# The gate job of one group of LayerNorm moments, and the GpSimd transfer behind it, one job later in the key sweep

## The chip, the core and the metric

The kernel runs on one core of a Trainium2 chip. A core has five engines with instruction streams of their own: PE (TensorE, the matmuls), DVE (VectorE), ACT (ScalarE), POOL (GpSimd) and SP (SyncE, which here only issues transfers). They wait for one another by semaphores. Transfers between the core's memory and DRAM are carried out by 16 DMA engines; SP, ACT and POOL only issue them. The metric is the device time of one execution in microseconds (us); the median of three runs is compared.

## The reference

The input `x` has 2048 rows (tokens) of 576 numbers. The output mixes two blocks with a gate per token:

```python
def _A_ref(x, wqkv, wo):                       # linear attention, 32 heads of 18
    q, k, v = split of (x @ wqkv) into heads
    pq, pk = phi(q), phi(k)                    # phi(t) = t+1 if t>0 else exp(t), + 1e-6
    kv  = einsum("bhsd,bhse->bhde", pk, v)     # sums over all tokens
    z   = einsum("bhsd->bhd", pk)
    o = einsum("bhqd,bhde->bhqe", pq, kv) / (einsum("bhqd,bhd->bhq", pq, z) + 1e-6)
    return o @ wo

def _B_ref(x, w1, b1, w2, b2):                 # per token: LayerNorm, Dense(4608), GELU, Dense(576)
    y = _layernorm(x)                          # (x - mean) / sqrt(var + 1e-5)
    return gelu(y @ w1 + b1) @ w2 + b2

g = sigmoid((x * gate_w).sum(-1, keepdims=True))
out = g * _A_ref(x, ...) + (1 - g) * _B_ref(x, ...)
```

## The kernel before

**Tiles and stages.** The 2048 tokens are 16 tiles of 128. The kernel first sweeps over the tiles (the key sweep, up to about 187 us of the span), then forms the attention weights, attends tile by tile, and spends the rest, from about 280 us to the end at 1120 us, in the two dense layers of block B, whose order a planner sets. Only the key sweep matters here. It visits the tiles in the order `ORDER`; below, step n is the n-th tile visited (n from 0), and the main loop runs steps 3 to 15.

**One step of the sweep** (the loop at L582). PE projects the tile on the key weights in two halves of 14 matmuls each (called KEY(n) below, 28 matmuls `ps<-y 128x288`), multiplies parts of step n-1 (`add_products`, `ps<-xs,ks` and `ps<-ks,xs`), projects on the query weights (again 28 matmuls `ps<-y`, called QUERY(n)), and adds the other products of step n-1. The two PSUM banks 6 and 7 take the halves in turn, KEY half 0, KEY half 1, QUERY half 0, QUERY half 1, so each half must be read out before the projection two halves later may write. The read-out of a half is two ACT activations (tile `e`) and one DVE instruction, `k<-ps,e` for keys and `accs<-ps,e` (or `acc<-ps,e`) for queries. ACT and DVE also split the next `x` tile (`y<-t`), the finished keys (`ks<-k`) and the tile in its other layout (`xs<-xn`) into a high and a low part; ACT takes the sum of squares of step n-1 (`xn<-xn,nmean`).

**Transfers.** SP issues, in program order, the next `x` tile (`t<-in_xm`, `t<-in_xe` twice; three steps ahead), its row layout (`xn<-in_x`; one step ahead) and what the jobs below ask for. SP issues in order: what waits holds up all behind it. Each of SP's transfers uses one of eight semaphores in turn and waits until the transfer eight places ahead has landed.

**The jobs.** Between the pieces of a step three lists of small jobs are run: list 3n behind `split_xn` of step n and ahead of QUERY(n)'s read-out, list 3n+1 behind that read-out, list 3n+2 at the step's end, ahead of KEY(n+1)'s read-out. They are written into each engine's stream in that place. Two sorts of jobs matter.

*Gates* (L347 to L385): for a group b of tiles (`MOMENTS`, L34; group 0 is the first two tiles visited, group 1 the third and fourth, and so on) `gates_in` (three DVE instructions of two columns), `gates_act` (on ACT: an Exp, a Sqrt and an Exp, with two loads of function tables), `gates_out` (eight small DVE instructions) and `share_moments`, in which POOL issues a transfer that writes the group's means and reciprocal deviations (tile `mr`, 128 partitions of four numbers) to DRAM (`moments`), turned around so that each of the 512 numbers goes to a place of its own.

*Pairs* (`Y_JOBS`, L83): for a pair j of tiles `load_pair` has SP load the pair's moments back, repeated in all partitions (`accs<-moments`), and the tiles themselves (`accs<-in_xm`, `accs<-in_xe` twice, for each of the two tiles). `normal_pair` (DVE, four instructions `accs<-accs 128x768`) normalizes them, then sums, splits (`ys`, `y`) and stores (`yd<-ys`) follow, for block B. Pair 0 needs group 0's moments: it is loaded in list 13 and normalized in lists 16 (two instructions) and 17 (two). Pair 1 needs group 1's: loaded in list 20, normalized in 22 and 23.

The list number of each group's gates is set in L561; list 12 belongs to step 4 and list 15 to step 5:

```python
    for b, n in enumerate((9, 12, 22, 28)):
        at(n, gates_in, b)
        at(n + 1, gates_act, b)
        at(n + 2, gates_out, b)
        at(n + 2, share_moments, b)
```

All instructions go through a helper, so the profile gives nearly all of them line L111; they are told apart by their tiles.

Of the kernel before, what the change touches and what calls it, by code (L numbers as in the profile page):

```python
# [114 lines left out]
def tile_gated_mix(ctx: ExitStack, tc: tile.TileContext, x, xm, xe, wm, we, wvm, wve, wo, um, ue, w2, b1, b2, gw, out):  # L115
# [68 lines left out]
    for part in (KEY, QUERY):  # L184
        for half in range(2):
            n = HALF + 2 * (part == KEY and half)
# [360 lines left out]
    def at(n, f, *args):  # L547
        jobs[n].append(lambda: f(*args))
# [9 lines left out]
    at(3 * 5, sp.dma_start, b1s, b1)  # L558
    at(9, load_wv)
    at(40, load_wo)  # L560
    for b, n in enumerate((9, 12, 22, 28)):  # L561
        at(n, gates_in, b)
        at(n + 1, gates_act, b)
        at(n + 2, gates_out, b)
        at(n + 2, share_moments, b)
# [956 lines left out]
```

## Time and profile before

| | us |
|---|---|
| median of three runs | 1126.16 (1124.97 to 1127.82) |
| the profiled execution, its own time | 1122.1 |
| its span | 1120.4 |
| PE busy in the span | 1105.2 |
| mean granted TensorE clock | 0.998 |

The profile is of one execution. Its span begins with the first instruction. "Idle before" is time in which an engine waited, with what ended the wait. In a timeline the number behind x tells how many equal instructions a row merges, so that a row's duration can hold more than one of them. DMA rows have two sides: the row on SPq or POOLq is the issue, and the transfer lands later. PE is busy nearly throughout, so what counts is the few places at which it isn't, and the granted clock behind them.

### The profile page before, as it was taken

The numbers are of one execution on the slowest core, as the hardware profiler recorded it, in microseconds if no ns is written. First come the engines' busy times: TensorE is split into PE (matmuls) and PEld (weight loads), VectorE is DVE, ScalarE is ACT, GpSimd is POOL, SyncE is SP. The second block draws the span as 40 slices with busy tenths as digits, with TensorE's granted clock in tenths as the row PEclk, the third lists the DMA queues.
The fourth block names the chain that finished last, engine by engine and source line by source line (L and its number), as shares of the span: only waits on it lengthen the run. The fifth ranks groups of instructions, "written<-read, shape, count | busy, mean of one in ns | idle before, by whom it ended". The sixth has DMA issues, their size and how long they took to land.

```text
span 1120.4 us, 18589 instructions
## 1 busy us (share of the span) xinstructions
PE 1105.2 (99%) x6766; PEld 1007.0 (90%) x6766; DVE 890.9 (80%) x1381; ACT 648.4 (58%) x1158; POOL 396.2 (35%) x326
## 2 busy tenths in 40 slices
PE   9989999999999999999999999999999999999998
PEld 9989999999888888898988889888999899889898
DVE  5558785796787979879988987887887788878888
ACT  6657765354556665676756666445554555455542
POOL 2111112431334252544515353325443444344430
PEclk9999999999999999999999999999999999999999
DMA  6475673745636546473564649774445444444432
GB/s 184 122 94 177 165 202 110 265 176 193 202 133 209 194 162 202 143 268 118 209 211 156 225 155 349 291 250 130 117 127 146 126 120 127 137 127 127 119 111 85
DMA packets 108862, 189.42 MB, mean 169 GB/s; under 512 B 8924, under 2 KB 68588, under 8 KB 104674
## 3 DMA queue, kind: packets, MB, share of 16 engines
q1 hardware_dynamic: 107858, 187.49, 52.7%
q8 instruction: 53, 0.87, 0.3%
q10 hardware_dynamic: 720, 0.74, 0.2%
q14 instruction: 39, 0.32, 0.1%
q0 software_dynamic: 192, 0.01, 0.0%
HBM read 121.40 MB, written 66.80 MB: 168 GB/s over the span
## 4 chain that ended last, share of the span: by engine, by line
PE 80%; DVE 10%; DMA 4%; issue 2%; ACT 2%; SPq 1%; POOL 1%; ACTq 0%; DVEq 0%; POOLq 0%
PE ps L111 80%; DVE accs L111 3%; DVE h L111 2%; DVE region L111 1%; DMA accs<-in_xe 1%; SPq L111 1%; DVE wa L111 1%; DMA w1d<-wb 1%; DMA fresh<-in_ue 1%; DVE wb L111 1%; DVE u L111 1%; POOL fresh L111 1%; ACT u L111 0%; DMA s<-in_wm 0%; DMA fresh<-in_w 0%
## 5 line engine op out<-in xcount | busy, mean ns | idle before, releaser
L111 PEld LDWEIGHTS ps<-region,h 128*128 128x128 f32 x3144 | 454.8, 188 | 43.5 <-DVE accs L111 7.2
L111 PE MATMUL ps<-region,h 128*128 128x288 f32 x3144 | 479.4, 295 | 5.4 <-DVE accs L111 2.3
L111 DVE TENSOR_TENSOR accs<-ps,accs 128x576 f32<-128x576 f32 x336 | 250.5, 753 | 88.4 <-PE ps L111 83.7
L111 POOL TENSOR_TENSOR fresh<-fresh 128x288 f32<-128x288 f32 (+1 forms) x164 | 172.2, 1057 | 374.2 <-DMA fresh<-in_w 258.2
L111 PE MATMUL ps<-y,wa 128*128 128x512 f32 x1008 | 269.0, 393 | 0.4 <-DVE wa L111 0.4
L111 PE MATMUL ps<-y,wb 128*128 128x512 f32 x756 | 203.9, 396 | 0.2 <-ACT u L111 0.2
L111 PEld LDWEIGHTS ps<-y,wa 128*128 128x128 f32 x1008 | 176.7, 188 | 25.5 <-DVE wa L111 1.1
L111 POOL TENSOR_TENSOR u<-u 128x512 f32<-128x512 f32 x104 | 163.3, 1570 | 96.9 <-DVE h L111 59.4
L111 DVE TENSOR_TENSOR h<-u,h 128x512 fp32r<-128x512 f32 x222 | 187.3, 858 | 3.7 <-ACT u L111 3.0
L111 PEld LDWEIGHTS ps<-y,wb 128*128 128x128 f32 x756 | 132.6, 188 | 23.4 <-ACT u L111 0.8
L111 PE MATMUL ps<-y 128*128 128x288 f32 (+1 forms) x896 | 127.5, 299 | 4.7 <-DVE k L111 4.3
L111 PEld LDWEIGHTS ps<-y 128*128 128x128 f32 x896 | 123.9, 191 | 6.8 <-DVE k L111 4.7
L111 ACT ACTIVATE u<-ps 128x512 f32<-128x512 f32 x73 | 43.7, 599 | 145.2 <-PE ps L111 145.2
L111 DVE TENSOR_TENSOR region<-fresh,region 128x576 fp32r<-128x576 f32 x120 | 97.1, 809 | 2.0 <-ACT region L111 1.6
L111 ACT ACTIVATE region<-fresh 128x576 fp32r<-128x576 f32 x120 | 74.1, 630 | 36.7 <-PE ps L111 31.9
L111 ACT ACTIVATE h<-ps,b1s 128x512 fp32r<-128x512 f32 x45 | 30.9, 686 | 77.0 <-PE ps L111 76.9
L111 ACT ACTIVATE h<-u,b1s 128x512 fp32r<-128x512 f32 x73 | 52.6, 721 | 32.0 <-DVE u L111 31.2
L111 ACT ACTIVATE h<-u 128x512 fp32r<-128x512 f32 x104 | 60.3, 620 | 16.1 <-POOL u L111 16.0
L111 PE MATMUL ps<-wp,qt 128*128 128x288 f32 x448 | 63.3, 298 | 0.0
L111 DVE TENSOR_TENSOR wa<-fresh,wa 128x512 fp32r<-128x512 f32 x64 | 47.9, 749 | 18.8 <-ACT wa L111 17.9
L111 DVE TENSOR_TENSOR u<-ps,u 128x512 f32<-128x512 f32 x74 | 50.9, 688 | 14.8 <-ACT u L111 12.8
L111 POOL TENSOR_TENSOR pks<-pks,k 128x576 f32<-128x576 f32 x15 | 21.9, 1459 | 111.8 <-DVE k L111 111.8
(122 smaller groups left out, 1040.7 us busy)
## 6 DMA issues: line engine op xcount, KB each, us to landing
w1d<-wa SPq DMA_DIRECT2D x17, 1280.0 KB
wa<-w1d SPq DMA_DIRECT2D x68, 320.0 KB
fresh<-in_w SPq DMA_DIRECT2D x70, 288.0 KB
y<-yd SPq DMA_DIRECT2D x14, 1280.0 KB
w1d<-wb SPq DMA_DIRECT2D x17, 960.0 KB
wb<-w1d SPq DMA_DIRECT2D x51, 320.0 KB
yd<-ystage SPq DMA_DIRECT2D x28, 320.0 KB
fresh<-in_um SPq DMA_DIRECT2D x64, 128.0 KB
```

Source lines behind the costliest of these rows:

```text
L111: return lambda *args, **kwargs: self.tc.keep_in_program_order(op(*args, **kwargs))
```

## The change

One number of L561: the jobs of group 1 go from lists 12, 13 and 14 (all in step 4) to lists 13, 14 and 15. The transfer by POOL goes from list 14 to list 15, which is in step 5.

```diff
-    for b, n in enumerate((9, 12, 22, 28)):
+    for b, n in enumerate((9, 13, 22, 28)):
         at(n, gates_in, b)
         at(n + 1, gates_act, b)
         at(n + 2, gates_out, b)
         at(n + 2, share_moments, b)
```

No instruction is added or removed. The streams of PE, ACT and SP stay as they were, word for word; DVE's and POOL's change. In the rows below `mr_108` is group 1's tile, `moments_113` and `moments_114` are groups 0 and 1 in DRAM.

DVE at the end of step 4: `gates_in` of group 1 (the three rows without a sign), then what stands behind it.

```order
+L111 SCALAR_TENSOR_TENSOR accs<-ps,e 128x288 x2
 L111 COPY mr_108<-nmean 128x2
 L111 TENSOR_SCALAR mt<-sumsq 128x2
 L111 TENSOR_SCALAR g<-gsum 128x2
-L111 SCALAR_TENSOR_TENSOR accs<-ps,e 128x288 x2
+L111 SCALAR_TENSOR_TENSOR k<-ps,e 128x288
+L111 TENSOR_TENSOR y<-t,y 128x512
+L111 TENSOR_TENSOR y<-t,y 64x128
+L111 SCALAR_TENSOR_TENSOR k<-ps,e 128x288
+L111 SCALAR_TENSOR_TENSOR ks<-k,ks 128x576
+L111 TENSOR_TENSOR xs<-xn,xs 128x512
+L111 TENSOR_TENSOR xs<-xn,xs 128x64
```

`gates_in` stood ahead of the two read-outs of QUERY(4) and now stands behind them; behind it DVE goes on at once with step 5.

DVE at the end of step 5: the last instruction of group 1's `gates_out`, and what follows it, up to `normal_pair` of pair 0 (the last row).

```order
 L111 TENSOR_SCALAR mt<-mt 128x2
 L111 TENSOR_TENSOR mr_108<-mr_108,mt 128x2
-L111 SCALAR_TENSOR_TENSOR k<-ps,e 128x288
-L111 TENSOR_TENSOR y<-t,y 128x512
-L111 TENSOR_TENSOR y<-t,y 64x128
-L111 SCALAR_TENSOR_TENSOR k<-ps,e 128x288
-L111 SCALAR_TENSOR_TENSOR ks<-k,ks 128x576
-L111 TENSOR_TENSOR xs<-xn,xs 128x512
-L111 TENSOR_TENSOR xs<-xn,xs 128x64
 L111 SCALAR_TENSOR_TENSOR accs<-ps,e 128x288 x2
 L111 TENSOR_TENSOR accs<-accs 128x768 x4
```

`gates_out` stood ahead of step 5's seven key-side instructions and now stands behind them, directly ahead of the read-outs of QUERY(5) and of pair 0's normalizing.

POOL: the running sum of the keys (`pks`, one instruction a step) and the transfers of the moments.

```order
 L111 TENSOR_TENSOR pks<-pks,k 128x576
 L111 DMA moments_113<-mr_107 128x4x1
-L111 TENSOR_TENSOR pks<-pks,k 128x576
+L111 TENSOR_TENSOR pks<-pks,k 128x576 x2
 L111 DMA moments_114<-mr_108 128x4x1
-L111 TENSOR_TENSOR pks<-pks,k 128x576 x4
+L111 TENSOR_TENSOR pks<-pks,k 128x576 x3
 L111 DMA moments_115<-mr_109 128x4x1
```

The transfer of group 1 moved behind step 5's key sum; group 0's stays where it was.

## The prediction

> **What bounds the kernel now.** I read the chain of waits first, then who waits for whom in the key sweep, then the timelines of PE, DVE and SP where PE stands still, and the transfers by windows last. The page's chain, and the longest waits of PE and of DVE for a transfer between 30 and 230 us (us in total, times, longest):
>
> ```profile
> PE 80%; DVE 10%; DMA 4%; issue 2%; ACT 2%; SPq 1%; POOL 1%; ACTq 0%; DVEq 0%; POOLq 0%
> PE ps L111 <- DVE k L111: 4.3, 1, 4.3
> DVE accs L111 <- DMA accs<-in_xe: 6.1, 2, 5.8
> ```
>
> PE is the bound; in the whole sweep it stands still once. PE's timeline shows where (start, us; the 28 matmuls `ps<-y` are KEY or QUERY):
>
> ```profile
> 61.20 3.90 PE L111 MATMUL ps<-y 128*128 128x288 f32 x28
> 66.69 3.88 PE L111 MATMUL ps<-y 128*128 128x288 f32 x28
> 72.40 3.90 PE L111 MATMUL ps<-y 128*128 128x288 f32 x28
> ...
> 82.40 5.46 PE L111 MATMUL ps<-y 128*128 128x288 f32 x28 [4.35 <-DVE k L111]
> 89.69 3.90 PE L111 MATMUL ps<-y 128*128 128x288 f32 x28
> 100.89 3.90 PE L111 MATMUL ps<-y 128*128 128x288 f32 x28
> 112.09 3.90 PE L111 MATMUL ps<-y 128*128 128x288 f32 x28
> ```
>
> KEY(5) starts at 61.20, KEY(6) at 72.40, KEY(7) at 89.69, KEY(8) at 100.89, KEY(9) at 112.09. A step takes 11.20 us, but step 6 takes 17.29. So 6.09 us are lost in it: 4.35 us of idle PE ahead of QUERY(6), and 1.58 us more because QUERY(6) takes 5.46 us instead of 3.88 (the rest, 0.16, is between the two readings). The second part is the clock, by the window that holds QUERY(6) (the 0.57 is the granted clock):
>
> ```profile
> 82.00:86.00 4.00, 3.60 (x16) 3.60 (x17) 3.11 (x6) 2.08 (x3) 1.42 (x1) 0.57 0.22 69
> ```
>
> The cause of the idle time, followed back: the chain's own row, and DVE's instruction that ends PE's wait.
>
> ```profile
> 66.57 13.33 DMA accs<-in_xe
> 81.90 0.46 DVE k L111
> ```
>
> QUERY(6) waits for a bank that DVE reads out at 81.90 (`k<-ps,e`); ahead of it in DVE's stream stands `normal_pair` of pair 0, which waits for the pair's last `accs<-in_xe`, 13.33 us on its way. Why so slow? Here are POOL's four transfers of moments (groups 0 to 3), the time from issue to landing of the four, and windows of 5 to 8 us with the DMA engines' busy share and the GB/s moved as their last two numbers:
>
> ```profile
> 51.98 0.82 POOL L111 DMA_DIRECT2D moments<-mr  x1 [6.17 <-DVE mr L111]
> 63.19 0.78 POOL L111 DMA_DIRECT2D moments<-mr  x1 [6.17 <-DVE mr L111]
> 111.43 0.77 POOL L111 DMA_DIRECT2D moments<-mr  x1 [2.99 <-DVE mr L111]
> 134.38 0.77 POOL L111 DMA_DIRECT2D moments<-mr  x1 [2.99 <-DVE mr L111]
> DMA to landing us min/median/max: 10.5/11.6/12.7
> ```
>
> ```profile
> 56.00:64.00 8.00, 8.00 (x59) 7.87 (x58) 4.25 (x16) 6.27 (x13) 1.80 (x2) 1.00 0.82 25
> 64.00:68.00 4.00, 4.00 (x27) 3.69 (x26) 2.30 (x5) 3.66 (x10) 1.21 (x1) 1.00 0.95 165
> 68.00:76.00 8.00, 8.00 (x59) 7.87 (x58) 2.48 (x5) 3.34 (x8) 0.21 (x1) 1.00 0.70 36
> 90.00:98.00 8.00, 8.00 (x57) 7.69 (x57) 6.31 (x13) 6.39 (x15) 1.44 (x1) 1.00 0.82 236
> 118.00:123.00 5.00, 5.00 (x37) 4.89 (x36) 3.82 (x9) 3.23 (x7) 1.11 (x1) 1.00 0.83 27
> 139.00:145.00 6.00, 6.00 (x41) 5.71 (x41) 4.79 (x10) 4.47 (x12) 1.43 (x1) 1.00 0.71 28
> ```
>
> Four times, from 4 to 7 us behind POOL's issue until 11 to 13 us behind it, everything moves at 25 to 36 GB/s with engines 70 to 83% busy; between these stretches it is 165 to 236. I call this the stretch of a group. Group 1's (issue 63.19, stretch to 76) falls on pair 0's loads, which SP issues from 62.98 on:
>
> ```profile
> 62.98 0.34 SPq L111 DMA_DIRECT2D accs<-moments  x1
> ...
> 68.39 7.60 SPq L111 DMA_DIRECT2D t<-in_xm  x1
> ```
>
> SP itself is caught behind them: 7.60 us on `t<-in_xm` for step 8, and all that it issues next. (The 62.98 is not group 1's doing: the first row waits for group 0's moments, issued 11.0 us before.)
>
> **The change, part by part.** *`gates_in` and `gates_act`.* `gates_in` goes behind the read-outs of QUERY(4), so ACT's first Exp waits for it. Groups 2 and 3 already stand in this phase of a step; the nearest rows are group 2's Exp and, in the second fence, group 3's end of step 10 with KEY(11) and KEY(12), which has `gates_out`, two read-outs and four normalizing instructions in the order that step 5 gets:
>
> ```profile
> 100.72 0.20 ACT L111 ACTIVATE g<-g 128x2 f32<-128x2 f32 x1 [0.74 <-DVE g L111]
> ```
>
> ```profile
> 134.51 4.01 PE L111 MATMUL ps<-y 128*128 128x288 f32 x28
> 145.82 3.90 PE L111 MATMUL ps<-y 128*128 128x288 f32 x28
> 134.74 3.80 DVE L111 TENSOR_TENSOR accs<-accs 128x768 f32<-128x768 f32 x4
> 138.46 0.45 DVE L111 SCALAR_TENSOR_TENSOR k<-ps,e 128x288 f32<-128x288 f32 x1
> ```
>
> ACT waits 0.74 us; queued behind it are KEY(8)'s read-out and all of ACT's next step. Yet KEY(8) to KEY(9) is 11.20 us: a plain step. Cost 0; its cover is PE's work between KEY's first half and QUERY's, and without it the cost would be those 0.74 us.
>
> *`gates_out`.* Eight instructions move behind step 5's key side; QUERY(5)'s read-outs wait for them, and KEY(6) for these. KEY(11) to KEY(12) takes 11.31 us in that order: 0.11 us over a plain step. I take 0.11; the ends are 0 (the row of KEY(8)) and 0.74.
>
> *The transfer on POOL.* It goes past one key sum, which nobody waits for soon. Group 2's left 10.54 us behind its step's KEY (111.43 - 100.89), so group 1's would leave at 61.20 + 10.54 = 71.7. Its stretch, now from 67 or 68 to 76, is then from 75 or so to 71.7 + 12.7 = 84.4.
>
> *Pair 0's loads.* SP's order is unchanged and group 0's landing too, so they leave from 62.98 as before. By the shapes in the code the pair is 1.02 MB (256 KB of repeated moments, and 256 and twice 64 KB for each tile). Up to 68 us 0.66 MB have been moved (165 GB/s for 4 us); at 236 GB/s the rest is there by 69.6, at 165 by 70.2. In step 10 DVE reached `normal_pair` 0.23 us behind KEY(11)'s start (134.74 - 134.51), so here at about 72.6. So DVE's wait of 6.1 us goes whole; KEY(6) is read out 3.95 us behind its start as KEY(11) was (138.46), and QUERY(6) starts 5.49 us behind KEY(6) as QUERY(5) did (66.69 - 61.20).
>
> *What is late next.* Behind pair 0 SP issues step 8's `x` tile (0.32 MB), step 6's row layout `xn` (0.29 MB) and step 9's tile (0.32 MB). At 236 GB/s from 69.6 on, `xn` is there at 72.2, ahead of the stretch. ACT's use of `xn` in steps 6 and 7:
>
> ```profile
> 84.45 0.67 ACT L111 ACTIVATE xs<-xn 128x576 fp32r<-128x576 f32 x1
> ...
> 95.95 0.68 ACT L111 ACTIVATE xs<-xn 128x576 fp32r<-128x576 f32 x1
> ```
>
> In step 7 that is 6.26 us behind KEY(7), so in step 6 it would be at 72.40 + 6.26 = 78.7. Step 9's tile may be caught; it has until step 8. Step 7's `xn` is issued into the stretch at about 78 and lands by 85 or 86 (0.29 MB at 236 GB/s behind its end); step 7 uses it at 83.7 + 6.26 = 90.0. Then pair 1: SP waits for group 1's landing, 84.4 at the latest, instead of issuing at 89.29, less the 6.0 that everything is earlier, or 83.3.
>
> ```profile
> 89.29 0.41 SPq L111 DMA_DIRECT2D accs<-moments  x1
> 100.60 3.81 DVE L111 TENSOR_TENSOR accs<-accs 128x768 f32<-128x768 f32 x4
> ```
>
> That leaves 100.60 - 6.0 - 84.4 = 10.2 us until its normalizing, against 11.3 that were enough, and the 4.3 to 6.2 us that 1.02 MB take at 236 or 165 GB/s. Cost 0.
>
> *Sum.* 17.29 - 11.20 - 0.11 = 5.98 us less in step 6, all of it on PE's path, and nothing in the streams behind is tied to an absolute time: 1122.1 - 6.0 = 1116.1 us for the profiled execution. It lies 4.1 us below the median of the runs; applied to that, 1126.2 - 6.0 = 1120.2. No row tells what those 4.1 us are; were they a longer wait at the same place, the gain could reach 10 us.
>
> **The skill, weighed.** The page "DMA: Bandwidth & Descriptors" of the Trainium skill, in its section on the anatomy of one DMA on the SWDGE (gpsimd) path, gives such a transfer 2.0 us and its bytes at 436 GB/s. By that, the 2 KB of a group would be gone 2 us after the issue, the slow stretches would not be theirs, and the change would gain nothing (the third rival); the 10.5 to 12.7 us measured here decide against it. The page "TensorE: Matmul & The Clock Gate", in its section on what is actually happening, has the clock halve after an idle window of about 3.4 us. Pair 0's 4.35 us idle with its 0.57 agrees, and by that rule a rest of the wait under 3.4 us would cost only itself.
>
> **The rivals.** *First, a rest of the wait stays:* pair 0 lands 1 to 4 us after 72.6, or `xn` is caught in part. DVE has little room in step 6, so most of it comes back on PE: gain 2 to 5 us, 1121.2 to 1124.2. For it: SP's semaphores let a late transfer hold the eighth behind it. Against: 2.4 us between landing and need.
>
> *Second, the stretch hits step 6's `xn` whole, and the kernel gets slower.* The transfer then lands when the stretch ends, 84.4; from ACT's use of it (84.45) to KEY(7) (89.69) there are 5.24 us of work, so KEY(7) would start at 89.6, and with the 1.58 us of the slow clock the sweep would stand 1.5 us worse than now: 1127.7. It is slower from a landing of 82.9 on, and by 0.3% (3.4 us, about what a measurement of this kernel can tell from no change) from 86.3 on. For it: group 1's issue at 71.7 comes before the 72.2 at which `xn` has landed, and only the 4 to 7 us from issue to stretch keep them apart. Against: group 3's issue at 134.38 stood 2.6 us behind an `xn` (131.75), and KEY(11) to KEY(12) is 11.31 us:
>
> ```profile
> 131.75 0.52 SPq L111 DMA_DIRECT2D xn<-in_x  x1
> ```
>
> *Third, the stretches aren't the transfers':* pair 0's loads are slow by themselves, and nothing changes: 1126.2. Against: four stretches for four issues, and pair 1's loads at 236 GB/s.
>
> **How the numbers follow.** Forecast 0.73 (1118.5 to 1121.5 by itself), first rival 0.11, second 0.09, third 0.07. Faster by over 0.3% is the forecast and half of the first rival: 0.78. Slower by over 0.3% is the second with a landing beyond 86.3, and something unforeseen: 0.07. The rest, 0.15, is within. The range goes from 1116.5 (part of the unexplained 4.1 us gained as well) to the far end of the first rival, 1124.2.
>
> **What would show it.** Right: PE has no wait for `k` near 78 us and the clock stays at 1.00; KEY(6) to KEY(7) takes about 11.3 us; `normal_pair` follows the read-outs without a wait; a stretch at 25 to 40 GB/s lies between 75 and 84 instead of 68 and 76. Wrong: ACT waits at `xs<-xn` for the transfer near 79 us (the second rival), or DVE at pair 0's `normal_pair` in spite of full speed before 72 (the third), or DVE there by a few us or at pair 1's near 94 (the first).

## The result, and the profile after

The changed kernel is faster, by less than 1%. In the first comparison its median is 1116.43 us (1116.29 to 1119.06), that of the kernel before 1125.57 (1124.13 to 1127.82), four runs each: a ratio of 0.9923, with a 95% interval from 0.9900 to 0.9945. In later sets with far more runs, on three chips, the gain is smaller: 0.9974 [0.9963, 0.9985] and 0.9970 [0.9956, 0.9984] on the two that ran both kernels (below). Two executions were disturbed and are left out of all figures below: one of 2189.58 us in e5, and one of 5120.93 us in e9, the one that was profiled there.

| profiled execution | before | after |
|---|---|---|
| its own time, us | 1122.1 | 1116.29 |
| its span, us | 1120.4 | 1114.6 |
| mean granted clock | 0.998 | 1.000 |
| KEY(6) to KEY(7), us | 17.29 | 11.20 |

The span is 5.8 us shorter. Followed by the start of PE's n-th matmul, which is the same matmul in both traces, the kernel before is 0.5 us ahead up to KEY(6), 5.6 us behind from KEY(7) on (89.69 against 84.07), and 5.8 us behind at the last matmul. So in this pair of traces the whole gain lies in step 6.

PE's longest wait between 30 and 230 us, and its timeline (start, us; KEY(5), QUERY(5), KEY(6), QUERY(6), KEY(7), KEY(8)):

```profile
PE ps L111 <- DVE wp L111: 0.2, 1, 0.2
```

```profile
61.67 3.90 PE L111 MATMUL ps<-y 128*128 128x288 f32 x28
67.16 3.88 PE L111 MATMUL ps<-y 128*128 128x288 f32 x28
72.87 3.90 PE L111 MATMUL ps<-y 128*128 128x288 f32 x28
78.36 3.88 PE L111 MATMUL ps<-y 128*128 128x288 f32 x28
84.07 3.90 PE L111 MATMUL ps<-y 128*128 128x288 f32 x28
95.27 3.90 PE L111 MATMUL ps<-y 128*128 128x288 f32 x28
```

The 4.35 us ahead of QUERY(6) are gone, QUERY(6) takes 3.88 us at full clock instead of 5.46, and each of these steps is a plain one of 11.20 us. The 0.2 us that is left belongs to another place (`wp`).

The rows of the other engines on which the prediction's steps stood, from the timelines of ACT (the Exp of group 1, and step 6's use of `xn`), DVE (`normal_pair` of pair 0 and of pair 1), POOL (group 1's transfer) and SP (pair 1's moments), and the time from issue to landing of the four transfers of moments:

```profile
61.50 0.20 ACT L111 ACTIVATE g<-g 128x2 f32<-128x2 f32 x1 [0.74 <-DVE g L111]
79.12 0.68 ACT L111 ACTIVATE xs<-xn 128x576 fp32r<-128x576 f32 x1
72.58 3.81 DVE L111 TENSOR_TENSOR accs<-accs 128x768 f32<-128x768 f32 x4
94.97 3.81 DVE L111 TENSOR_TENSOR accs<-accs 128x768 f32<-128x768 f32 x4
72.22 0.78 POOL L111 DMA_DIRECT2D moments<-mr  x1 [2.99 <-DVE mr L111]
83.88 0.41 SPq L111 DMA_DIRECT2D accs<-moments  x1
DMA to landing us min/median/max: 10.1/10.5/10.8
```

And the windows, with granted clock, DMA share and GB/s as the last three numbers:

```profile
68.00:76.00 8.00, 8.00 (x58) 7.87 (x58) 7.22 (x17) 3.79 (x9) 2.02 (x2) 1.00 0.74 199
76.00:84.00 8.00, 8.00 (x53) 7.57 (x52) 6.80 (x15) 6.51 (x15) 1.42 (x1) 1.00 0.51 22
84.00:90.00 6.00, 6.00 (x42) 5.67 (x41) 4.94 (x11) 4.31 (x11) 0.35 (x1) 1.00 0.79 271
```

From 68 to 76 us, where the kernel before moved 36 GB/s, 199 are moved now: pair 0's loads and the `xn` of step 6 pass ahead of the stretch. The slow stretch has gone behind the transfer, to 76 to 84 us (22 GB/s), and there nothing that is in flight is needed soon: DVE's `normal_pair` at 72.58 and ACT's `xs<-xn` at 79.12 show no wait for a transfer.

### The profile page after: what moved, and what is told of

Same layout as the page of the kernel before. It is cut to its first block, busy times and chain, and to the rows that moved or that the text cites. A ratio compares the mean times of both kernels' runs of the same rounds, so it can differ in the third digit from the quotient of the medians.

```text
span 1114.6 us, 18587 instructions
## 1 busy us (share of the span) xinstructions
PE 1102.9 (99%) x6766; PEld 1004.2 (90%) x6766; DVE 890.6 (80%) x1381; ACT 647.6 (58%) x1158; POOL 398.2 (36%) x326
## 4 chain that ended last, share of the span: by engine, by line
PE 77%; DVE 11%; DMA 5%; ACT 2%; issue 2%; SPq 2%; POOL 1%; ACTq 0%; DVEq 0%; POOLq 0%
PE ps L111 77%; DVE accs L111 3%; DVE h L111 2%; DVE region L111 2%; SPq L111 2%; DMA w1d<-wb 1%; DMA fresh<-in_ue 1%; DVE wb L111 1%; ACT u L111 1%; DVE wa L111 1%; DMA yd<-ystage 1%; DMA accs<-in_xe 1%; DVE u L111 1%; ACT h L111 1%; POOL u L111 0%
## 5 line engine op out<-in xcount | busy, mean ns | idle before, releaser
L111 DVE TENSOR_TENSOR region<-fresh,region 128x576 fp32r<-128x576 f32 x120 | 99.5, 829 | 2.1 <-ACT region L111 1.7
```

Of the source, the lines that this page charges most:

```text
L111: return lambda *args, **kwargs: self.tc.keep_in_program_order(op(*args, **kwargs))
```

## The experiments

The theory on trial: group 1's transfer of 512 four-byte pieces slows all DMA traffic for up to 8 us; in the kernel before these fall on pair 0's loads; DVE waits for them in order, PE waits for DVE, and the clock falls. Rivals: that something else of the change removes the wait (the places of `gates_in` and `gates_out`); that GpSimd's way of issuing, not the pieces, is at fault; that the loads are slow by themselves. The kernel before was run many times beside each set: median 1120.07 us with e1 to e4 (31 runs), 1120.04 with e5 to e8 (35), 1121.00 with e9 to e11 (24), on three chips. What was expected of e1 to e4 was worked out from the first comparison, and its sizes came out too large.

### e1: the kernel before, unchanged

> The kernel before, unchanged, profiled once more, to see where the 4 us lie by which its runs (1124 to 1128 us) exceed its profiled execution (1122.1), and with them the 3 us by which the measured gain (9.1 us) exceeds the 6.0 of the sum. If the wait for pair 0's loads simply has another length in each execution, step 6 (KEY(6) to KEY(7)) takes 19 to 23 us in an execution of 1124 to 1128 us instead of the 17.29 of the first profile, and all other steps 11.2 to 11.3. If the extra time lies elsewhere, step 6 takes 17 to 17.5 us again and another place shows it.

Measured: 1119.38 us (1117.15 to 1123.24), ratio 0.9999 [0.9984, 1.0014]. In its profile, QUERY(6) and KEY(7):

```profile
80.90 3.99 PE L111 MATMUL ps<-y 128*128 128x288 f32 x28 [1.71 <-DVE k L111]
87.66 4.00 PE L111 MATMUL ps<-y 128*128 128x288 f32 x28 [0.75 <-DVE accs L111]
```

```profile
66.70 11.70 DMA accs<-in_xe
```

KEY(6) began at 73.53, so step 6 took 14.13 us: the loss is there, but it is 2.93 us and not 6.09, nor any size that was expected. PE waits at the same place for the same read-out, 1.71 us instead of 4.35, then 0.75 us ahead of KEY(7), and the clock doesn't fall. By the chain (the last row) pair 0's last load was 11.70 us on its way, against 13.33 in the first profile. The loss of the first profile is thus no constant. (The profile puts DVE's first wait at pair 0, 3.12 us, down to a `t<-in_xe`, which `normal_pair` does not read; as the transfers take their semaphores in turn, that name is doubtful.) And yet this execution's span (1121.3 us) is longer than the first profile's (1120.4): against the profile of e5 it is already 1.0 us late ahead of step 6, 4.1 us behind it, and between 320 and 730 us, in the dense layers, it falls back by another 2.7. In the three profiles of the kernel before (e6 below is the third) this part differs by up to 3 us; the time of one execution can't tell a gain of this size.

### e2: the transfer alone, one list later

```diff
     for b, n in enumerate((9, 12, 22, 28)):
         at(n, gates_in, b)
         at(n + 1, gates_act, b)
         at(n + 2, gates_out, b)
-        at(n + 2, share_moments, b)
+        at(n + 2 + (b == 1), share_moments, b)
```

> Only POOL's transfer of group 1 goes to list 15; the gates stay in lists 12 to 14, so DVE and ACT run as before. By the theory of the stretch the whole gain is there: POOL issues right behind step 5's key sum, near 68.3 instead of 71.7, its stretch is from 72 or 73 to 80, pair 0's loads have landed by then, and step 6 takes 11.2 to 11.5 us: 9 us (7 to 10) below the kernel before, unless the earlier stretch catches step 6's row layout, which would show as a wait at that tile. By the rival that the place of the gates on DVE and ACT is what counts, nothing is gained: 0 to 1 us.

Measured: 1118.17 us (1115.94 to 1119.33), ratio 0.9979 [0.9968, 0.9989], which is 1.9 us where 7 to 10 were expected. POOL issues at 68.24, because with `gates_out` in its old place nothing holds it any longer. The rows: POOL's issue; what ACT waits for in step 6; KEY(7).

```profile
68.24 0.78 POOL L111 DMA_DIRECT2D moments<-mr  x1
80.98 0.69 ACT L111 ACTIVATE xs<-xn 128x576 fp32r<-128x576 f32 x1 [2.11 <-DMA xn<-in_x]
85.01 4.01 PE L111 MATMUL ps<-y 128*128 128x288 f32 x28 [1.15 <-DVE accs L111]
```

DVE's wait at pair 0 is gone, so the gates' places were not what removed it. But the stretch (35 GB/s from 72 to 76 us) now catches the next transfer in SP's order, step 6's `xn`, which in the chain of waits is 11.42 us on its way. KEY(6) began at 72.49, so the step takes 12.52 us and loses 1.32. This is the prediction's second rival, in a mild form: an issue 4.0 us earlier than the changed kernel's is too early.

### e3: the changed kernel, with a second transfer at the old time

```diff
+    def share_again():
+        pool.tensor_copy(four, acc[ORDER[4]][:, HALF:HALF + 4])
+        for _ in range(2):
+            pool.memset(kvs, 0.0)
+        pool.dma_start(nowhere.rearrange("a (t n) -> n (a t)", n=P), four)
...
+    at(14, share_again)
```

> The changed kernel with one more transfer of the same form by POOL into a place that nobody reads, issued near 63.5 us, where group 1's stood before; POOL reaches it through one small copy that waits for step 4 and two memsets of 1.06 us. By the theory of the stretch pair 0's loads are slow again: a stretch from 68 to 76 at 20 to 40 GB/s, DVE waits 5 us or more at normal_pair, step 6 takes 16 us or more, and the gain is lost: 0 to 3 us slower than the kernel before, since group 1's own stretch now follows. By the rival that the place of the gates is what counts, it stays at the time of the changed kernel, 8 to 9 us below the kernel before.

Measured: 1120.35 us (1116.98 to 1125.61), ratio 1.0009 [0.9988, 1.0030] to the kernel before: the gain is gone. The added transfer is issued at 63.57 us; nothing reads what it writes. The window that in the changed kernel's profile moves 196 GB/s, then QUERY(6), ACT's use of `xn` and KEY(7):

```profile
68.00:72.00 4.00, 4.00 (x30) 3.94 (x30) 3.30 (x12) 2.76 (x6) 1.16 (x1) 1.00 0.60 40
```

```profile
79.03 3.98 PE L111 MATMUL ps<-y 128*128 128x288 f32 x28 [0.52 <-DVE k L111]
82.32 0.69 ACT L111 ACTIVATE xs<-xn 128x576 fp32r<-128x576 f32 x1 [1.14 <-DMA xn<-in_x]
86.35 4.01 PE L111 MATMUL ps<-y 128*128 128x288 f32 x28 [1.34 <-DVE accs L111]
```

With everything else of the change in place, one more transfer at the old time brings the stretch, DVE's wait for pair 0 (2.1 us, where 5 or more were expected) and a step 6 of 13.49 us (from 72.86; 16 or more expected) back. The loss of 2.29 us is near e1's 2.93, in other shares: PE waits 0.52 us ahead of QUERY(6) and 1.34 ahead of KEY(7). The transfer is the cause, and its time decides.

### e4: the kernel before, group 1's transfer in 128 pieces of 16 bytes

```diff
-        pool.dma_start(moments[b].rearrange("a (t n) -> n (a t)", n=P), mr[b].rearrange("p a t -> p (a t)"))
+        to = moments[b].rearrange("a (t n) -> n (a t)", n=P)
+        if b == 1:
+            to = moments[b].rearrange("a (q e) -> (a q) e", e=4)
+        pool.dma_start(to, mr[b].rearrange("p a t -> p (a t)"))
```

> The kernel before with everything in its old place, but group 1's transfer is written so that the four numbers of a partition lie side by side (128 pieces of 16 bytes instead of 512 of 4). The moments of group 1 are then in the wrong order in DRAM, and pair 1 is normalized with wrong numbers of the same shape; no other work changes. If it is the 512 separate pieces that make the stretch, its length falls to about a quarter (2 us or so), pair 0 lands by 72 to 73, and step 6 takes 11.2 to 13 us: 6 to 9 us below the kernel before. If any transfer by POOL to DRAM makes such a stretch, whatever its pieces, nothing changes: within 1 us of the kernel before.

Measured: 1117.01 us (1116.06 to 1119.18), ratio 0.9969 [0.9955, 0.9982], in the order of the kernel before: 3.1 us gained, where 6 to 9 were expected. The landing of the four transfers (group 1's is the 5.7), the window of the old stretch, KEY(6) and KEY(7):

```profile
DMA to landing us min/median/max: 5.7/9.1/10.4
68.00:72.00 4.00, 4.00 (x32) 3.98 (x31) 2.44 (x4) 2.41 (x5) 1.28 (x1) 1.00 0.64 170
73.45 3.90 PE L111 MATMUL ps<-y 128*128 128x288 f32 x28
...
84.65 3.90 PE L111 MATMUL ps<-y 128*128 128x288 f32 x28
```

The same 2 KB from the same engine at the old time (64.24), and no stretch: 170 GB/s, a step 6 of 11.20 us, no wait. What slows the traffic is the form in which the 2 KB go out, 512 pieces of 4 bytes. Whether their number, their size or their scattered places counts is not told apart, since e4 changes all three. The loads of pair 0 are not slow by themselves.

### e5 and e6: both kernels again, on another chip

> The changed kernel once more, beside a new profile of the kernel before on the same chip (next run). In the profiles so far the kernel before lost 6.09 us in step 6 in one (17.29 us) and 2.93 us in another (14.13), and their spans differ by some 3 us more or less in the dense layers behind the sweep. So step 6 takes 11.2 us here, and the gain is the wait of step 6 on this chip, 3 to 6 us, give or take 1: 0.3 to 0.6% below the kernel before, not the 0.8% of the first comparison, if its extra 3 us were chance in the dense layers; 9 us again if they belong to the change.

> The kernel before, to have its trace on this chip. Step 6 takes 14 to 17.5 us, all other steps 11.2 to 11.3; the loss in step 6 is the larger, the longer group 1's stretch: with the transfer landing 9.3 to 10 us behind its issue about 3 us, at 12.7 us behind it 6 us.

Measured: the changed kernel 1117.83 us, ratio 0.9974 [0.9963, 0.9985]; the kernel before, as a copy, 1121.72, ratio 1.0007 [0.9991, 1.0023]. In the profile of the changed kernel all steps around the change take 11.20 us. In that of the kernel before, QUERY(6), KEY(7), pair 0's last load in the chain, and a window:

```profile
80.60 5.50 PE L111 MATMUL ps<-y 128*128 128x288 f32 x28 [2.09 <-DVE k L111]
...
87.94 3.90 PE L111 MATMUL ps<-y 128*128 128x288 f32 x28
...
65.80 12.31 DMA accs<-in_xe
```

```profile
82.00:84.00 2.00, 2.00 (x10) 2.00 (x10) 1.22 (x1) 2.00 (x4) 1.42 (x1) 0.50 0.00 0
```

KEY(6) began at 72.86: step 6 takes 15.08 us and loses 3.88. PE stood still for only 2.09 us, little more than in e1, but this time the granted clock falls to 0.50 and QUERY(6) takes 1.6 us longer.

### e7: the kernel before, the same pieces issued by SP

```diff
-        pool.dma_start(moments[b].rearrange("a (t n) -> n (a t)", n=P), mr[b].rearrange("p a t -> p (a t)"))
+        by = sp if b == 1 else pool
+        by.dma_start(moments[b].rearrange("a (t n) -> n (a t)", n=P), mr[b].rearrange("p a t -> p (a t)"))
```

> The kernel before, but SP issues group 1's transfer instead of POOL, in the same 512 pieces of four bytes. SP reaches it behind pair 0's loads, near 68 us, where POOL issued it in the run that moved the transfer alone (68.24; step 6 took 12.52 us there, with a wait for step 6's row layout). If the pieces make the stretch, it is the same here: a stretch at 20 to 40 GB/s from 72 or so to 78 or 80 us, a wait at step 6's row layout, step 6 at 12 to 14 us. If it is the way by which POOL issues, there is no stretch, and step 6 takes 11.2 us.

Measured: 1120.91 us (1115.15 to 1123.38), ratio 1.0000 [0.9983, 1.0017]. SP reaches the issue at 67.58. A window, ACT's use of `xn` and KEY(7):

```profile
72.00:76.00 4.00, 4.00 (x29) 3.94 (x28) 3.93 (x5) 1.09 (x3) 0.00 (x0) 1.00 0.61 39
```

```profile
82.45 0.69 ACT L111 ACTIVATE xs<-xn 128x576 fp32r<-128x576 f32 x1 [3.28 <-DMA xn<-in_x]
86.48 5.39 PE L111 MATMUL ps<-y 128*128 128x288 f32 x28 [2.31 <-DVE accs L111]
```

The same stretch (39 GB/s) without GpSimd: the issuing engine isn't at fault. With an issue near e2's the harm is of e2's kind, `xn` late by 3.28 us, and step 6 takes 13.67 us (KEY(6) at 72.81). The step's loss of 2.47 us holds only up to KEY(7); KEY(7) itself then runs at the lower clock.

### e8: group 1 three lists later than in the changed kernel

```diff
-    for b, n in enumerate((9, 12, 22, 28)):
+    for b, n in enumerate((9, 16, 22, 28)):
```

> The gates of group 1 three lists further on (16 instead of 13), the transfer in list 18, near 82.5 us. Pair 0 is as safe as in the changed kernel and step 6 costs at most 1 us more (gates_out now stands ahead of QUERY(6)'s read-out). But SP waits for group 1's landing at pair 1's load, until 92 to 95 us instead of 83.9, and behind it stand pair 1's tiles and step 8's row layout. So the wait comes back one step later: DVE waits 2 to 6 us at pair 1's normal_pair (95 us), and steps 7 and 8 together take 24 to 29 us instead of 22.4: 2 to 7 us slower than the changed kernel, about the time of the kernel before. If pair 1 had room for that, it would stay within 1 us of the changed kernel.

Measured: 1124.55 us (1122.99 to 1126.53), ratio 1.0036 [1.0023, 1.0048]: slower than the kernel before. POOL issues at 83.66. Below are the first and the last of `gates_out`'s eight instructions and the read-outs of QUERY(6) on DVE; SP's issue of pair 1's moments; DVE at pair 1; then PE's two waits and KEY(9).

```profile
81.94 0.16 DVE L111 TENSOR_SCALAR g<-g 128x2 f32<-128x2 f32 x1
...
83.20 0.16 DVE L111 TENSOR_TENSOR mr<-mr,mt 128x2 f32<-128x2 f32 x1
...
85.34 0.81 DVE L111 SCALAR_TENSOR_TENSOR accs<-ps,e 128x288 f32<-128x288 f32 x2
...
94.65 0.33 SPq L111 DMA_DIRECT2D accs<-moments  x1
101.09 1.95 DVE L111 TENSOR_TENSOR accs<-accs 128x768 f32<-128x768 f32 x2 [4.13 <-DMA accs<-in_xe]
```

```profile
85.85 4.01 PE L111 MATMUL ps<-y 128*128 128x288 f32 x28 [1.37 <-DVE accs L111]
...
105.99 5.51 PE L111 MATMUL ps<-y 128*128 128x288 f32 x28 [3.17 <-DVE k L111]
113.33 3.90 PE L111 MATMUL ps<-y 128*128 128x288 f32 x28
```

Two costs. `gates_out` (1.4 us from 81.94 on) now stands ahead of the read-outs in the fullest stretch of DVE's step 6, PE waits 1.37 us for these, and step 6 takes 12.74 us (73.11 to 85.85). And pair 1's loads, held by group 1's landing, leave at 94.65 instead of 83.88: DVE waits 4.13 us, and step 8 takes 16.17 us (97.16 to 113.33). Together 1.54 + 4.97 = 6.5 us are lost to the changed kernel. Less the 2.9 to 3.9 us that e1 and e6 lose in step 6, that is 2.6 to 3.6 more than the kernel before; measured are 4.0 to 4.5 by the ratio and the medians, where about the time of the kernel before was expected.

### e9, e10 and e11: a third chip, and no stretch at all

e9 is the kernel before, e10 the changed kernel; e11 is the changed kernel with all four transfers in 16-byte pieces:

```diff
-        pool.dma_start(moments[b].rearrange("a (t n) -> n (a t)", n=P), mr[b].rearrange("p a t -> p (a t)"))
+        pool.dma_start(moments[b].rearrange("a (q e) -> (a q) e", e=4), mr[b].rearrange("p a t -> p (a t)"))
```

> The kernel before, profiled a fourth time, to see what goes with the size of its loss. So far step 6 took 17.29, 14.13 and 15.08 us, where the slowest of the four transfers of moments landed 12.7, 11.4 and 11.8 us behind its issue. If the loss follows the stretch, a landing under 11.5 us gives under 15 us for step 6, one over 12.3 gives over 16.

> The changed kernel beside it on the same chip: step 6 takes 11.2 us again, whatever the stretch, and the medians differ by the loss of the run above, give or take 1.5 us.

> The changed kernel, with all four transfers by POOL written in pieces of 16 bytes (all moments of block B's first half are then in the wrong order in DRAM; the work is the same). What the stretches still cost in the changed kernel: PE waits 0.2 us in the sweep, so there is nothing to gain there: within 0.5 us of the changed kernel. If slow transfers in the sweep still cost something that no wait shows, it gains more than 1 us.

Measured: e9 1120.91 us, ratio 1.0000 [0.9988, 1.0012], with no trace of its step 6 that could be used, so what was expected of it stays untested; e10 1117.43 (1114.32 to 1119.21), ratio 0.9970 [0.9956, 0.9984]; e11 1116.95 (1115.97 to 1118.54), ratio 0.9969 [0.9957, 0.9981]. The landings and the window of group 0's stretch, of e10 first and then of e11:

```profile
DMA to landing us min/median/max: 9.4/9.5/9.5
56.00:64.00 8.00, 8.00 (x58) 7.87 (x58) 3.11 (x8) 5.58 (x11) 0.94 (x1) 1.00 0.74 41
```

```profile
DMA to landing us min/median/max: 1.7/2.9/3.7
56.00:64.00 8.00, 8.00 (x57) 7.83 (x57) 3.29 (x9) 5.59 (x12) 1.42 (x1) 1.00 0.63 189
```

In e11 the transfers land in 1.7 to 3.7 us and no stretch is left, and yet it is only 0.5 us below e10, with intervals that overlap almost wholly. PE waits for none of them in either. In the changed kernel the three other stretches, and group 1's in its new place, cost nothing that can be measured, and there was no more to be had here. (A version with larger pieces and the moments in the right order was not made, since e11 leaves nothing for it to gain.)

## Why the prediction was right, and where not

**Right, step by step, in the traces.** The wait that was to go was the right one, and its cause was: e3 brings it back with the transfer alone, e4 takes it away with the transfer alone. *`gates_in`, `gates_act`:* ACT waits 0.74 us at 61.50, as group 2's row had it, and the step costs PE nothing. *`gates_out`:* 0.11 us were taken, 0 are measured (72.87 to 84.07 is 11.20). *POOL's transfer* was put at 10.54 us behind KEY(5); it leaves 10.55 behind (72.22 - 61.67). *The stretch* was put at 75 to 84.4; the slow window is 76 to 84. *Pair 0:* `normal_pair` at about 72.6, measured 72.58, without a wait. *`xn`:* used 6.25 us behind KEY(6), where 6.26 were taken, without a wait. *Pair 1:* SP issues at 83.88, where 84.4 at the latest was given, and 11.1 us are left until its normalizing (94.97), where 10.2 at least were given. The sum for the profiled execution, 1116.1 us, met 1116.29. That it met so closely is luck in part: step 6 takes 11.2 us in e10 too, and the profiled execution there took 1117.76. *The loads* were put too fast: 236 GB/s were taken for those behind pair 0, and 199 are measured from 68 to 76 us. SP issued step 6's `xn` at 71.26, and its 0.29 MB take 1.5 us at that rate, so it was not there at the 72.2 of the prediction; the room behind it was large enough.

**Mis-sized: the step from the profiled execution to the medians.** The prediction subtracted the same 6.0 us from the median of the runs, and got 1120.2. Measured is 1116.43, 0.07 us below the range; the gain in the medians is 9.1 us. In the later sets it is only 2.2 us (1120.04 - 1117.83) and 3.6 us (1121.00 - 1117.43). The step that failed is to take step 6's loss for a constant. It was 6.09, 2.93 and 3.88 us in three profiles of the same kernel, with group 1's transfer, the slowest of the four in each, landing 12.7, 11.4 and 11.8 us behind its issue, and pair 0's last load 13.33, 11.70 and 12.31 us on its way. Every run also has a mean granted clock. On the three chips 26 of the 90 runs of the kernel before have 0.998 or less, and their median is 1122.43 us; the other 64 have 0.999 or 1.000, and a median of 1119.96. Every one of the changed kernel's 21 runs on two of these chips has 1.000, and the median is 1117.62. So by these medians the change is worth some 2.3 us where the kernel before keeps its clock, as in e1's trace, and some 4.8 us where it loses it, as in the two other traces. The profile that the prediction was worked out from was one of the costlier kind.

**Open: the other 3 us of the first comparison.** Its four runs of the kernel before (1124.13 to 1127.82) all lie above the highest of the 90 (1124.09; one run of e6's copy took 1124.65), and above the profiled execution of the same kernel (1122.1). The prediction named the 4.1 us between the two as unexplained and allowed that they might be gained as well; in that comparison they were. Runs of that length do come with a transfer at the old time: three of e3's ten took 1125.3 to 1125.6 us, with a granted clock of 0.997. No trace was taken of any of these, so whether it was a longer wait at the same place, with slower landings still, or something in the layers, is not settled.

**The rivals.** *The third*, that the stretches aren't the transfers', falls with e3 and e4. *The second*, that `xn` is hit, is a real mechanism: it came in e2 and e7, with an issue at 68.24 and 67.58, and left a loss of 1.32 and 2.47 us in the step. It did not make these kernels slower than before, because `xn` was late by 2.1 and 3.3 us and no more. In the changed kernel only 4.0 us of a later issue keep it away; the prediction's 0.09 for it was not too much. *The first*, a rest of the wait at pair 0 or at pair 1, came only in e8, where pair 1 was caught instead. The prediction's list of what is late next had pair 1 as the place to look at, with 10.2 us of margin, and e8 shows that a change three lists later than this one uses it up.

**A sentence that fell.** From the Trainium skill's page "TensorE: Matmul & The Clock Gate" (section "What's actually happening") the prediction drew that a rest of the wait under some 3.4 us would cost only itself. The traces disagree. PE was idle for 2.09 us in e6, 2.31 in e7 and 3.17 in e8, and the 28 matmuls behind it took 5.50, 5.39 and 5.51 us; behind 1.15, 1.34, 1.37 and 1.71 us (e2, e3, e8, e1) they took 3.99 to 4.01. So a rest of 2 us could already have cost some 1.5 us more. Where the idle time falls counts as well. In each of the four traces in which the clock fell during the sweep, it is 0.50 for one stretch of 3.41 us, and its changes lie whole multiples of 3.41 us apart (75.09 us at full clock ahead of the fall in the first profile and in e6, 81.92 in e7, 102.40 in e8). In the 3.41 us just ahead of the fall PE was idle for 3.41, 2.09, 2.02 and 2.78 us (first profile, e6, e7, e8); on the same grid an edge cuts e1's 1.71 us into 1.05 and 0.66, and e8's 1.37 us ahead of KEY(7), which lie within one such stretch, were not enough. No term of the sum hung on the sentence.

## What to carry to other kernels

When a load is slow, look at what else the DMA engines carry in that window: a tiny transfer made of hundreds of pieces of a few bytes can slow all traffic for up to 8 us, and its time of issue is then a lever as good as the form of its pieces. Move such a transfer to where the loads in flight have slack on both sides, and check both: four microseconds too early it hits the next load, three lists too late it makes its own reader wait. And where a loss hangs on a race between transfers, one profile doesn't give its size; profile the kernel before more than once, and use the mean granted clock of each run as a cheap sign of whether the clock fell (not of the whole time: e1's profiled execution has 1.000 and took 1123.05 us).

## What the runs showed of the hardware

- Writing 2 KB to DRAM as 512 pieces of 4 bytes takes 8.8 to 12.7 us from issue to landing and brings everything on the 16 DMA engines down to 22 to 41 GB/s in the windows shown, which are 4 to 8 us long. As 128 pieces of 16 bytes it takes 1.7 to 3.7 us when all four are so written, and 5.7 us in e4, and the traffic beside it stays at 170 to 189 GB/s. The Trainium skill's page "DMA: Bandwidth & Descriptors" (section "Anatomy of one DMA — SWDGE (gpsimd) path") gives such a transfer about 2.0 us, by a formula without a term for the number of pieces: e11's 1.7 to 3.7 us lie about it, and the four-byte pieces miss it by 6.8 us and more.
- It is the same from SP's queue as from GpSimd's: 39 GB/s in e7.
- PE's clock fell to 0.50 for 3.41 us, and the next 28 matmuls lost 1.5 to 1.6 us, where PE had been idle for 2.02 us or more of the 3.41 us just ahead (e6, e7, e8 and the first profile). It did not fall with 1.37 us idle in such a stretch (e8, ahead of KEY(7)). Where in between the bound lies, no run shows.
- Step 6's loss differs by a factor of two between three executions of the same kernel (2.93, 3.88, 6.09 us), with group 1's transfer of moments landing 11.4 to 12.7 us behind its issue.
